# Block-sparse attention and a gated convolution on one core: the first group's output from split words, under a new order of work

## The chip, the cores and the metric

The kernel runs on one core of a Trainium2 chip. The metric is device time in microseconds (us) of one execution; three runs of the kernel before gave 233.24, 233.26 and 234.01, median 233.26. The engines are TensorE (PE, with its weight loads as PEld), VectorE (DVE), ScalarE (ACT), GpSimd (POOL) and SyncE (SP, which issues all DMAs here).

## The reference

Attention over local windows and block summaries, then a gated projection. Four batches, 8 heads of 64, 768 positions; the weights of the second part come as 64-bit floats.

```
k_sum = k.reshape(B, H, nb, 32, D).max(axis=3)
v_sum = v.reshape(B, H, nb, 32, D).mean(axis=3)
scores = concat(local q.k within 16 positions, q.k_sum + log(32)) * scale
x = softmax(scores) @ concat(v, v_sum)          # -> (B, S, H * D)
gate_pre[s] = sum_k conv_w[k] * x[s + k - 4]    # 5 taps along the sequence
out = (sigmoid(gate_pre) * (x @ w_val)) @ w_out
```

## The kernel before, in words

The work is cut into 12 groups `g` (a batch and a third of the sequence, 256 positions, all heads) and 24 units `u` (a group and half of its heads). Unit `u` belongs to group `u // 2`; `r` is 0 or 1, a pair of heads in the unit.

Nothing is scheduled by a planner. A table of words, `ORDER`, is walked once, and each word calls a function that issues a few instructions; every engine takes its own in the order of the table and waits only where an operand isn't ready or a buffer isn't free. The words that matter here, with their engines:

- `W` (PE): a warm-up matmul on zeros, whose result nobody reads. There are 34.
- `Lk`, `Ln`, `Lu`, `Lv`, `Lq`, `Lwv`, `Lwo`, `Lc` (SP): loads. `ks` (DVE) takes key maxima, `kc` (POOL) copies them in between the keys.
- `s` (PE): scores of a unit, 16 matmuls for each `r`. `n` (DVE): mask and row minimum, two score passes. `e` (ACT): two exponentials with row sums. `rr`, `rv` (DVE): row sum and reciprocal. `m` (POOL): normalization. `t` (PE): transposes, `c` (ACT, `cd` on DVE): their copy out of PSUM.
- `x` (PE): attention output. `Y`, `Yd`, `Ya`: its copy to `xf`. `X`, `Xd`, `Xp`: the high word `xh` of `xf` as float32r on ACT, DVE or POOL. `Z` (POOL): the low word `xl = xf - xh`.
- `vp`, `vt`, `vc`, `vb`, `vbc`: value sums of batch 0 (DVE and POOL, into `vpad`), their transposition on PE (`vb_mm`) and the copy. `tv`, `vsp`, `vsc`: the same for later batches.
- `I`, `Id` (ACT or DVE), `T` (DVE), `G` (ACT): the convolution, one start and four taps for each `r`, and the gate (tanh).
- `v` (PE): `val`, x @ w_val. `gf` (DVE): gate times val. `gh`, `ghp` (ACT or POOL) and `gl` (POOL): its high and low word. `o` (PE): the output matmuls; `ob`, `obd`: scaling; `O`: store.
- `rbwo`, `shwo`, `orwo`: a quarter of the 64-bit w_out made into fp32 `wf` (ACT, DVE, DVE). `wcwo`, `wcpwo` (ACT or POOL): its high word as float32r. `wlwo` (POOL): its low word. The same with `wv` for w_val.

A product in split words is three matmuls, high times high, high times low and low times high, each a single pass. `FP32_G = (0,)` makes `val` of group 0, and `FP32_OUT = (0,)` the output of group 0, from fp32 operands instead: `out_mm` then takes `gf` and `wf` and writes one quarter of the sum at a time (`o0.0.0` to `o0.1.3`). The trace shows two records for such a matmul. All three weights of `wf` share one tile: w_out's `wf` overwrites w_val's. `out_mm` in split words takes for each of four `ci` first high times high and high times low, then all four low times high:

```
terms = [(gh(g)[:, ci, rows], w[:, ci, cols]) for ci in range(4) for w in (wh, wl)]
terms += [(gl(g)[:, ci, rows], wh[:, ci, cols]) for ci in range(4)]
```

Of the kernel before, what the change touches and what calls it, by code (L numbers as in the profile page):

```python
# [56 lines left out]
n0.0.1 n0.0.0 ks0.3 Mi kc0.1 kc0.3 cv e0.0.1 e0.0.0 W25 s0.1 W26 W27 W28 W29 W30 n0.1.1 n0.1.0
rbc e0.1.1 e0.1.0 s1.1 shc ks0.2 n1.1.0 rr0 shwv0 rv0 hal0 kc0.2 W31 s1.0 W32 m0.1 e1.1.0 rbwv0
vp1.1 n1.1.1 e1.1.1 n1.0.0 n1.0.1 e1.0.1 t0.1 W33 c0.1 e1.0.0 orwv0 vp0.1 vp1.0 vp0.0 rr1 m0.0
t0.0 vt2.0 vc0.1 vc1.0 vt2.1 s2.1 s2.0 vc0.0 vc1.1 orc rv1 vb0 m1.0 n2.0.0 n2.1.1 n2.0.1 n2.1.0  # L60
c0.0 e2.0.0 e2.0.1 rbwv1 t1.0 e2.1.1 e2.1.0 c1.0 shwv1 vbcd0 orwv1 s3.0 s3.1 rbwv2 Lk1.0 x0.1
x0.0 Y0 m1.1 vt2.2 wcpwv0 wlwv0 t1.1 v0.1.0.0 n3.0.0 n3.1.1 n3.1.0 rr2 shwv2 n3.0.1 orwv2 I0.1
T0.1.0 rv2 T0.1.1 ks1.0 e3.0.0 e3.1.0 I0.0 e3.1.1 e3.0.1 c1.1 vt3.0 vt3.1 vt3.2 vt3.3 vt3.4
vc3.0 vt2.3 vt2.4 vc2.1 m2.1 vc3.1 vc2.0 m2.0 kc1.0 Lq2 s4.1 s4.0 Lwv3 Lv1 Lk1.2 Lk1.1 T0.1.2
n4.0.0 n4.1.0 n4.0.1 T0.0.0 n4.1.1 T0.0.1 shwv3 rr3 v0.0.1.0 v0.1.1.0 vb1 t2.1 e4.1.0 vbc1 s5.1
s5.0 T0.1.3 rv3 n5.1.0 T0.0.2 n5.0.0 T0.0.3 e4.0.0 e4.1.1 c2.1 rbwv3 x1.0 x1.1 Lk1.3 G0 Y1
wcpwv2 I1.1 n5.1.1 orwv3 ks1.2 T1.1.0 n5.0.1 ks1.1 v0.0.0.0 t2.0 c2.0 e4.0.1 m3.1 wcpwv1 m3.0
wlwv1 wlwv2 kc1.1 hal1 wcpwv3 wlwv3 kc1.2 v0.1.1.1 I1.0 v0.1.0.1 v0.0.1.1 t3.1 t3.0 e5.0.0
e5.1.1 c3.1 e5.0.1 c3.0 e5.1.0 Lq3 F1 Lwo1 Lv2 Lu1.2 s6.1 s6.0 Lwo0 Lwo2 Lu1.0 Lq4 F2 x2.1 x2.0
x3.1 x3.0 v0.0.0.1 T1.0.0 rr4 T1.1.1 rv4 T1.0.1 ks1.3 T1.1.2 n6.0.1 T1.0.2 n6.1.0 T1.1.3 n6.0.0  # L70
n6.1.1 Y2 X3 X2 Y3 T1.0.3 shwo1 gf0.0 G1 rbwo1 m4.0 kc1.3 m4.1 Z2 Z3 s7.0 s7.1 t4.0 t4.1 I2.0
I2.1 e6.1.1 gf0.1 n7.0.1 n7.1.1 orwo1 e6.0.1 e7.0.1 rbwo0 c4.1 e6.1.0 c4.0 v1.1.0 v1.0.0 v1.0.1
v1.1.1 rr5 T2.0.0 n7.0.0 T2.1.0 rv5 T2.0.1 n7.1.0 T2.0.2 shwo0 T2.1.1 orwo0 T2.0.3 x4.0 x4.1
rbwo2 e7.1.1 Y4 e7.1.0 s8.1 s8.0 shwo2 T2.1.2 orwo2 T2.1.3 tv1.2 m5.0 tv1.0 m5.1 G2 Ya4 gf1.0
t5.0 Lwo3 Lu1.1 Lk2.0 Lk2.1 Lu1.3 Lv3 o0.0.0 o0.0.1 rbwo3 I3.1 shwo3 orwo3 t5.1 o0.0.2 o0.1.0
o0.0.3 e6.0.0 c5.1 c5.0 T3.1.0 n8.0.0 rr6 n8.1.1 T3.1.1 n8.1.0 n8.0.1 rv6 tv1.3 tv1.1 X4 wcpwo0
Z4 e8.0.0 e7.0.0 rr7 I3.0 ob0.0 x5.0 x5.1 s9.1 s9.0 rv7 Y5 e8.1.0 vsp1 vsc1 e8.0.1 o0.1.1 o0.1.2
o0.1.3 Lk2.2 Lq5 Lk2.3 O0.0 F3 e8.1.1 Lq6 Lv4 Lu2.0 F4 T3.0.0 n9.1.1 T3.0.1 T3.0.2 Ya5 T3.1.2
T3.1.3 T3.0.3 m6.1 m6.0 wcpwo1 m7.1 hal2 X5 Z5 G3 rr8 n9.1.0 rv8 gf1.1 I4.1 T4.1.0 n9.0.0 t7.1
t6.0 wcwo3 I4.0 m7.0 m8.1 c7.1 n9.0.1 c6.0 v2.0.1 v2.1.1 t6.1 c6.1 s10.0 s10.1 x6.0 x6.1 T4.0.0  # L80
T4.0.1 T4.0.2 T4.0.3 T4.1.1 T4.1.2 T4.1.3 gh1.1 e9.0.0 ob0.1 e9.1.1 G4 Y6 I5.0 v2.0.0 v2.1.0
wcpwo2 wlwo0 t7.0 I5.1 c7.0 wlwo3 gl1.1 wlwo1 wlwo2 gh1.0 gl1.0 n10.1.0 n10.1.1 n10.0.0 n10.0.1
Ya6 s11.1 s11.0 x7.1 x7.0 T5.0.0 e10.1.0 e9.0.1 e9.1.0 gf2.0 gh2.0 Y7 T5.0.1 ks2.1 T5.1.0 T5.1.1
T5.0.2 T5.1.2 T5.0.3 rr9 T5.1.3 X6 o1.0 ob1.0 G5 e10.1.1 I6.0 I6.1 e10.0.0 tv2.0 m8.0 ks2.0
kc2.0 kc2.1 hal3 gl2.0 o1.1 n11.0.0 Ya7 X7 gf2.1 T6.1.0 n11.1.1 T6.0.0 n11.1.0 T6.1.1 n11.0.1
t8.1 t8.0 c8.0 c8.1 e10.0.1 e11.0.1 e11.1.1 e11.0.0 ob1.1 ghp2.1 gl2.1 Z7 o2.1 x8.1 s12.1 T6.1.2
T6.0.1 T6.1.3 T6.0.2 rv9 ks2.2 x8.0 s12.0 Y8 e11.1.0 m9.0 hal4 m9.1 Z6 kc2.2 n12.0.0 T6.0.3 G6
Ya8 I7.0 ob2.1 I7.1 rr10 ks2.3 n12.1.0 n12.0.1 n12.1.1 T7.1.0 T7.0.0 rv10 rr11 T7.0.1 T7.1.1
T7.1.2 rv11 T7.1.3 o2.0 t9.0 t9.1 c9.1 c9.0 v3.1.1 kc2.3 x9.1 s13.0 s13.1 x9.0 e12.1.1 Lv5 Lq7
Lu2.1 Lk3.1 Lk3.3 F5 e12.0.0 e12.1.0 Y9 tv2.1 v3.1.0 v3.0.0 n13.1.1 T7.0.2 T7.0.3 G7 I8.1 I8.0  # L90
n13.0.0 n13.0.1 Ya9 n13.1.0 m10.1 m10.0 X9 m11.1 Lu2.2 tv2.2 Xp8 Z8 Z9 t10.1 t10.0 v3.0.1
e12.0.1 c10.1 e13.1.1 gf3.1 T8.0.0 cd10.0 T8.0.1 rr12 T8.1.0 rv12 T8.0.2 T8.0.3 T8.1.1 T8.1.2
T8.1.3 Lu2.3 O0.1 Lv6 s14.1 x10.0 s14.0 x10.1 Y10 ob2.0 gh3.1 hal5 m11.0 gl3.1 tv2.3 gf3.0
n14.0.0 Ya10 G8 I9.1 I9.0 e13.0.0 e13.0.1 n14.0.1 T9.1.0 Xd10 T9.1.1 T9.0.0 n14.1.0 e13.1.0 rr13
T9.0.1 n14.1.1 v4.0.0 v4.0.1 v4.1.0 v4.1.1 rv13 T9.1.2 t11.1 vsp2 t11.0 c11.1 c11.0 s15.1 s15.0
x11.1 x11.0 e14.0.1 vsc2 Y11 ghp3.0 m13.1 gl3.0 m13.0 m12.1 m12.0 gf4.0 T9.1.3 T9.0.2 T9.0.3
# [792 lines left out]
```

## Time and profile before

| | |
|---|---|
| median of 3 runs | 233.26 us (233.24 to 234.01) |
| profiled execution | 233.49 us |
| its span, first to last instruction | 231.7 us |
| PE busy | 224.4 us, 97% |
| DVE busy | 199.7 us, 86% |
| POOL busy | 169.0 us, 73% |
| ACT busy | 165.4 us, 71% |

Busy time counts instructions in flight, so a PE that is busy 97% isn't PE at its peak. A wait is put down to the engine that ended it. Times in the rows count from the first instruction of the execution.

### The profile page before, as it was taken

How to read it: one execution, taken by the hardware profiler on the slowest of the kernel's cores; microseconds unless marked ns; L12 is line 12 of the kernel's file. 1: busy time of each engine (PE TensorE's matmuls, PEld its weight loads, DVE VectorE, ACT ScalarE, POOL GpSimd, SP SyncE). 2: the span in 40 equal slices, each digit the busy share in tenths (PEclk: the TensorE clock that was granted, in tenths of full speed). 3: DMA queues.
4: the chain of work that ended last, by engine and by line, in shares of the span. 5: the costliest groups of instructions: out<-in, count | busy, mean ns of one | idle time of the engine just before them, and what ended most of it. 6: DMA issues, size and time to landing. Idle time of an engine off the chain costs nothing.

```text
span 231.7 us, 8482 instructions
## 1 busy us (share of the span) xinstructions
PE 224.4 (97%) x3210; PEld 191.9 (83%) x3210; DVE 199.7 (86%) x743; ACT 165.4 (71%) x564; POOL 169.0 (73%) x257
## 2 busy tenths in 40 slices
...
GB/s 246 380 419 413 319 335 327 367 305 361 246 315 76 340 271 100 355 312 184 253 94 171 133 171 187 42 11 74 239 143 233 48 141 0 3 0 48 0 226 91
DMA packets 16167, 46.20 MB, mean 199 GB/s; under 512 B 2272, under 2 KB 2528, under 8 KB 16128
## 3 DMA queue, kind: packets, MB, share of 16 engines
...
## 4 chain that ended last, share of the span: by engine, by line
PE 83%; DVE 11%; ACT 3%; issue 1%; POOL 0%; ACTq 0%; DVEq 0%; POOLq 0%
PE out L753 28%; PE val L713 25%; PE s L566 8%; PE pt L618 8%; PE x L629 7%; DVE g L685 4%; PE warm_out L335 3%; DVE sn L581 2%; PE x L647 2%; DVE wf L400 1%; DVE vpad L309 1%; ACT gt L692 1%; DVE ks L258 1%; PE vsp L355 1%; DVE gf L721 1%
## 5 line engine op out<-in xcount | busy, mean ns | idle before, releaser
L685 DVE SCALAR_TENSOR_TENSOR g<-xf,cwt,g 128x256 f32<-128x256 f32 x192 | 93.3, 486 | 7.3 <-ACT g L219 3.0
L594 ACT ACTIVATE p<-sn,nm 128x120 f32<-128x120 f32 x192 | 73.5, 388 | 8.9 <-DVE nm L581 7.6
L608 POOL TENSOR_TENSOR p<-p,ri 128x480 f32<-128x480 f32 x48 | 46.7, 987 | 14.6 <-DVE ri L604 11.6
L713 PE MATMUL val<-xh,wv 128*128 128x256 f32 x352 | 49.6, 284 | 0.0
L581 DVE CUSTOM_DVE_ANT_0 sn<-s,mask 128x120 f32<-128x120 f32 x192 | 43.7, 276 | 3.4 <-PE s L566 3.4
L753 PE MATMUL out<-wo,gh 128*128 128x512 f32 (+1 forms) x184 | 45.8, 390 | 0.3 <-ACT gh L726 0.3
L713 PEld LDWEIGHTS val<-xh,wv 128*128 128x128 f32 x352 | 44.3, 189 | 0.9 <-issue 0.2
L753 PEld LDWEIGHTS out<-wo,gh 128*128 128x128 f32 x184 | 32.4, 188 | 7.3 <-ACT gh L726 0.7
L669 POOL TENSOR_TENSOR xl<-xf,xh 128x512 fp32r<-128x512 f32 x22 | 28.2, 1287 | 12.6 <-ACT xh L656 6.9
L594 ACT ACTIVATION_READ_ACCUMULATOR p<-sn,nm 128x1 f32 x192 | 36.8, 192 | 0.0
L729 POOL TENSOR_TENSOR gl<-gf,gh 128x512 fp32r<-128x512 f32 x22 | 28.2, 1289 | 7.6 <-ACT gh L726 7.3
L621 ACT COPY pts<-pt 120x512 f32<-120x512 f32 x42 | 23.6, 578 | 10.1 <-PE pt L618 10.1
L692 ACT ACTIVATE gt<-g 128x512 f32<-128x512 f32 x24 | 14.3, 597 | 19.7 <-DVE g L685 19.7
L618 PE MATMUL pt<-ident,p 128*120 128x128 f32 x192 | 26.7, 274 | 1.3 <-POOL p L608 1.3
L713 PE MATMUL val<-xl,wv 128*128 128x256 f32 x176 | 27.6, 279 | 0.0
L286 POOL TENSOR_TENSOR vT<-vT 128x384 f32<-128x384 f32 (+3 forms) x44 | 25.0, 569 | 2.9 <-DMA vT<-in_vT_dram 0.3
L618 PEld LDWEIGHTS pt<-ident,p 128*120 128x120 f32 x192 | 21.7, 137 | 5.1 <-POOL p L608 2.2
L753 PE MATMUL out<-wo,gl 128*128 128x512 f32 (+1 forms) x92 | 23.8, 381 | 0.0
L566 PE MATMUL s<-k,q 64*64 64x120 f32 x704 | 23.3, 267 | 0.3 <-DVE g L685 0.3
L713 PEld LDWEIGHTS val<-xl,wv 128*128 128x128 f32 x176 | 23.6, 188 | 0.0
L566 PEld LDWEIGHTS s<-k,q 64*64 64x64 f32 x704 | 18.2, 133 | 3.0 <-issue 2.2
L219 ACT ACTIVATE ob<-out 128x512 f32<-128x512 f32 (+1 forms) x21 | 11.9, 574 | 11.2 <-PE out L753 7.2
...
## 6 DMA issues: line engine op xcount, KB each, us to landing
...
```

Source lines behind the costliest of these rows:

```text
L286: nc.gpsimd.tensor_tensor(dst, src[:, :, :n], src[:, :, n : 2 * n], ALU.add)
L566: nc.tensor.matmul(sp(u)[64 * e : 64 * e + 64, h, c * KW : c * KW + KW], qs[64 * h : 64 * h + 64, i * QT : i * QT + QT], ktile[b, pr][64 * ...
L581: nc.vector.tensor_tensor_reduce(sn(u)[:, n, :], sp(u)[:, h, c * KW : c * KW + KW], mask[:, mv, :], -1.0 / math.sqrt(D), 3.0e38, ALU.add, ...
L594: nc.scalar.activation(pr_(u)[:, n, :], sn(u)[:, n, :], AF.Exp, bias=nm(u)[:, n : n + 1], scale=-1.0, accum_out=rs(u)[:, n, 0:1],)
L608: nc.gpsimd.tensor_tensor(pr_(u)[:, w], pr_(u)[:, w], st["ri", u][:, w].unsqueeze(2).broadcast_to([P, TPU, KW]), ALU.mult,)
L618: nc.tensor.transpose(pt[:KW, i, :], pr_(u)[:, TPU * r + i, :], ident)
L621: (eng or nc.scalar.copy)(pts(u)[:, TPU * r : TPU * r + TPU], st.pop(("pt", u, r))[:KW])
L669: nc.gpsimd.tensor_tensor(xl(g)[:, two(hp), :], xf(g)[:, two(hp), HALO:], xh(g)[:, two(hp), :].bitcast(F32), ALU.subtract,)
L685: nc.vector.scalar_tensor_tensor(gp(u)[:, r], xf(g)[:, pr, o : o + SG], cwt[:, pr, o : o + 1], gp(u)[:, r], ALU.mult, ALU.add,)
L713: nc.tensor.matmul(pp[:, r], w, x, start=first and n == 0, stop=last and n == len(terms) - 1)
L729: nc.gpsimd.tensor_tensor(gl(g)[:, two(cp), :], grp["gf", g, cp], gh(g)[:, two(cp), :].bitcast(F32), ALU.subtract)
L753: nc.tensor.matmul(pp, x, w, start=start and n == 0, stop=stop and n == len(terms) - 1)
```

## The change

`FP32_OUT` becomes empty: the output of group 0 is made by the same 24 matmuls of split words (`o0.0`, `o0.1`) as that of the other groups, and `gh0`, `gl0` and both words of w_out come before it. `val` of group 0 stays in fp32. One new word, `shpwv`, takes the low bits of one quarter of w_val on POOL, with a multiplication by 2^-29 and a minimum in place of a shift. All words of `ORDER` stand in another order; some change engine (three `I` become `Id`, two `Y` become `Yd`, three `ob` become `obd`; `wcwo` is on ACT four times, not once). `v0_sum` gets an argument that no word uses.

```
-FP32_OUT = (0,)
+FP32_OUT = ()
...
 ORDER = """
-ez wz W0 W1 W2 W3 W4 W5 Mu Lk0.0 Lk0.1 Mm ks0.0 ks0.1 kc0.0 W6 W7 W8 W9 W10 W11 W12 W13 W14 W15
-W16 W17 W18 W19 W20 W21 s0.0 W22 W23 W24 Lk0.3 Lk0.2 Lc Lwv0 Ln1 Ln0 Ln2 Lq1 Lwv1 Lv0 Lwv2 Ln3
...
+wz W0 W1 W2 W3 W4 W5 W6 W7 W8 W9 Mu W10 W11 W12 W13 Lk0.0 Lk0.1 Mm ks0.0 ks0.1 ez cv kc0.0 hal0
+s0.0 Lk0.3 Lk0.2 Ln0 Lwv0 Lc Ln2 Ln1 Lq1 Lwv1 Ln3 Lv0 Lwv2 n0.0.0 n0.0.1 ks0.3 kc0.1 kc0.3 Mi
...
-    def v0_sum(i, h):
+    def v0_sum(i, h, n=BLK):
...
     def low_bits(eng, dst, raw):
         low = raw.rearrange("p (n two) -> p two n", two=2)[:, 0]
+        if eng is nc.gpsimd:
+            eng.tensor_scalar(dst.bitcast(U32), low, 2.0**-29, 7.0, ALU.mult, ALU.min)
+            return
         eng.tensor_scalar(dst.bitcast(U32), low, 29, None, ALU.logical_shift_right)
...
-    def w_low(nm, k):
+    def w_low(nm, k, eng=None):
         if wide:
             if nm == "wo":
                 low_put(f"wo{k}", DM, wraw[nm, k])
             else:
-                low_bits(nc.vector, wf[:, k], wraw[nm, k])
+                low_bits(eng or nc.vector, wf[:, k], wraw[nm, k])
...
-        ("wcp", w_head, pcast),
+        ("wcp", w_head, pcast), ("shp", w_low, nc.gpsimd),
```

PE around the output of group 0, before (`s` scores, `pt` transposes, `vsp` the transposed value sums of batch 1):

```order
L566 MATMUL s_977<-k_0_398,q_732 64x120 x8
L618 MATMUL pt_0_1018<-ident,p_684 120x128 x4
L753 MATMUL out_0_1036<-wf,gf_0_803 128x512 x2
L618 MATMUL pt_1_1046<-ident,p_684 120x128 x4
L753 MATMUL out_0_1036<-wf,gf_1_848 128x512
L753 MATMUL out_1_1052<-wf,gf_0_803 128x512
...
L566 MATMUL s_1132<-k_2_519,q_732 64x120 x8
...
L355 MATMUL vsp_1153<-ident,vsT_1_1077 24x128
...
L753 MATMUL out_1_1052<-wf,gf_0_803 128x512
L753 MATMUL out_1_1052<-wf,gf_1_848 128x512 x2
```

The same place on PE in the change:

```order
L632 MATMUL x_1_1067<-pts_1036,v_740 64x64 x2
L756 MATMUL out_0_1112<-wo,gh_784 128x512 x8
L756 MATMUL out_0_1112<-wo,gl_1058 128x512 x4
L569 MATMUL s_1148<-k_3_504,q_975 64x120 x8
L569 MATMUL s_1148<-k_2_506,q_975 64x120 x8
...
L355 MATMUL vsp_1165<-ident,vsT_1_1125 24x128
...
L756 MATMUL out_1_1180<-wo,gh_784 128x512 x8
L756 MATMUL out_1_1180<-wo,gl_1058 128x512 x4
```

The eight fp32 matmuls in three runs have become two runs of twelve; the first stands behind all of `x5`, the second, as before, behind `vsp1`.

POOL at the value sums of batch 1, before (`vT` and `vsT` are sums of values, `p` the normalization, `xl` a low word):

```order
L608 TENSOR_TENSOR p_684<-p_684,ri_919 128x480
L286 TENSOR_TENSOR vT_1_1025<-vT_1_1025 128x24x16
...
L286 TENSOR_TENSOR vsT_1_1077<-vT_1_1025 128x24
L437 CAST wo<-wf 128x512
L669 TENSOR_TENSOR xl_1086<-xf_973,xh_1083 128x512
L608 TENSOR_TENSOR p_845<-p_845,ri_1065 128x480 x2
```

The same place on POOL in the change:

```order
L611 TENSOR_TENSOR p_685<-p_685,ri_773 128x480 x2
...
L732 TENSOR_TENSOR gl_1058<-gf_1_873,gh_784 128x512
L732 TENSOR_TENSOR gl_1058<-gf_0_766,gh_784 128x512
L443 TENSOR_TENSOR wo<-wf,wo 128x512 x4
L286 TENSOR_TENSOR vT_1_981<-vT_1_981 128x24x16
...
L286 TENSOR_TENSOR vsT_1_1125<-vT_1_981 128x24
L659 CAST xh_1109<-xf_973 128x512
L672 TENSOR_TENSOR xl_1196<-xf_973,xh_1109 128x512
```

Two subtractions `gl` and the four subtractions of w_out now stand ahead of the last value sums `vsT_1` (`tv1.1`), which `vsp1` on PE reads.

## Rows read from the trace of the kernel before

**Rows 1.** The page: busy us, share of the span, instructions.

```profile
PE 224.4 (97%) x3210; PEld 191.9 (83%) x3210; DVE 199.7 (86%) x743; ACT 165.4 (71%) x564; POOL 169.0 (73%) x257
```

**Rows 2.** Stretches: their us, busy PE, PEld, DVE, ACT, POOL; clock, DMA.

```profile
9.26:54.29 45.03, 42.78 (x682) 33.74 (x681) 44.09 (x197) 43.04 (x164) 39.30 (x73) 1.00 0.97 355
13.67:54.01 40.34, 38.55 (x629) 31.63 (x626) 39.41 (x172) 38.59 (x143) 37.20 (x67) 1.00 0.96 348
24.80:60.75 35.95, 35.95 (x580) 28.68 (x581) 34.92 (x143) 34.55 (x126) 32.11 (x57) 1.00 0.95 336
60.75:187.91 127.16, 127.16 (x2063) 114.89 (x2062) 119.45 (x448) 98.74 (x337) 103.42 (x142) 1.00 0.55 176
187.91:207.07 19.16, 18.88 (x192) 17.54 (x190) 15.46 (x39) 10.31 (x28) 9.69 (x10) 1.00 0.08 29
```

**Rows 3.** The chain of waits: start us, us, engine and group.

```profile
1.53 6.77 PE warm_out L335 x22
...
24.34 0.43 DVE g L685
24.80 1.05 PE s L566 x32
...
31.75 1.06 PE val L713 x4
...
51.12 1.72 PE out L753 x4
...
53.27 2.61 PE out L753 x6
...
57.80 0.54 PE vsp L355 x4
58.34 2.58 PE out L753 x6
60.91 0.87 PE pt L618 x8
...
64.97 0.98 PE s L566 x32
...
187.91 0.60 ACT ob L219
188.51 0.48 ACT xh L656
188.99 0.77 ACT p L594 x4
```

**Rows 4.** Timeline of DVE: start us, us, instruction, idle time before it.

```profile
8.94 0.28 DVE L581 CUSTOM_DVE_ANT_0 sn<-s,mask 128x120 f32<-128x120 f32 x1 [2.23 <-PE s L566]
```

**Rows 5.** Timelines of ACT and PE at the last wait.

```profile
205.92 0.59 ACT L656 CAST xh<-x 128x512 fp32r<-128x512 f32 x1 [0.61 <-PE val L713]
206.40 0.62 ACT L726 CAST gh<-gf 128x512 fp32r<-128x512 f32 x1
...
207.07 0.50 PE L753 MATMUL out<-wo,gh 128*128 128x512 f32 x1 [0.29 <-ACT gh L726]
```

**Rows 6.** Timelines of PE and POOL at the start.

```profile
1.53 5.04 PE L335 MATMUL warm_out<-warm 128*128 128x512 bf16 x14 [1.53 <-POOL warm L330]
...
5.29 0.44 POOL L272 COPY k<-ks 128x84 f32<-128x84 f32 x2 [3.26 <-DVE ks L258]
```

**Rows 7.** Timeline of POOL: first normalization, last copy in front of `vb1`.

```profile
13.67 1.93 POOL L608 TENSOR_TENSOR p<-p,ri 128x480 f32<-128x480 f32 x2 [0.68 <-DVE ri L604]
...
27.46 0.32 POOL L312 COPY vpad<-vpad 128x12 f32<-128x12 f32 x2
```

**Rows 8.** The chain of waits: 24 output matmuls of split words in a row.

```profile
72.26 5.71 PE out L753 x24
```

**Rows 9.** Groups by line on POOL: busy us, mean ns of one.

```profile
L729 POOL TENSOR_TENSOR gl<-gf,gh 128x512 fp32r<-128x512 f32 x22 | 28.2, 1289 | 7.6 <-ACT gh L726 7.3
...
L440 POOL TENSOR_TENSOR wo<-wf,wo 128x512 fp32r<-128x512 f32 x4 | 5.1, 1294 | 0.0
...
L437 POOL CAST wv<-wf 128x512 fp32r<-128x512 f32 x4 | 2.4, 610 | 0.0
```

**Rows 10.** Timelines of ACT (end of `c5`) and POOL (end of `tv1.1`).

```profile
53.31 1.08 ACT L621 COPY pts<-pt 120x512 f32<-120x512 f32 x2
...
53.78 0.23 POOL L286 TENSOR_TENSOR vsT<-vT 128x24 f32<-128x24 f32 x1
```

More of the change, by code (lines that the diff above doesn't have):

```diff
@@ L54 @@
 ORDER = """
-ez wz W0 W1 W2 W3 W4 W5 Mu Lk0.0 Lk0.1 Mm ks0.0 ks0.1 kc0.0 W6 W7 W8 W9 W10 W11 W12 W13 W14 W15
-W16 W17 W18 W19 W20 W21 s0.0 W22 W23 W24 Lk0.3 Lk0.2 Lc Lwv0 Ln1 Ln0 Ln2 Lq1 Lwv1 Lv0 Lwv2 Ln3
[L57 to L96, printed above, removed]
@@ L127 @@
-v9.0.1 v9.0.0 T19.0.3 n23.0.1 T19.1.0 n23.1.1 e23.1.1 Xd21 rr22 T19.1.1 T19.1.2 T19.1.3 e23.0.1
-G19 Z21 Z20 v9.1.0 v10.0.0 v10.0.1 v9.1.1 gf9.0 I20.0 T20.0.0 T20.0.1 rr23 I20.1 T20.1.0 rv23
-Lv11 F11 O7.0 O8.0 O6.1 ghp9.0 m23.0 t23.0 o8.1 T20.0.2 rv22 m22.1 T20.0.3 T20.1.1 T20.1.2
-T20.1.3 G20 Id21.0 I21.1 gf10.0 c23.0 T21.1.0 T21.0.0 T21.1.1 T21.0.1 T21.0.2 T21.1.2 gf9.1
-T21.1.3 T21.0.3 m23.1 hal11 gl9.0 m22.0 t22.1 t23.1 c22.1 c23.1 v10.1.0 t22.0 c22.0 x23.0 x23.1
-Yd23 X23 Z23 x22.0 x22.1 G21 Yd22 Id22.1 X22 gh9.1 gl9.1 ob8.1 v10.1.1 o9.0 Z22 v11.0.1 T22.1.0
@@ new lines @@
+e0.0.0 e0.0.1 W14 W15 W16 W17 W18 s0.1 W19 W20 W21 W22 n0.1.0 n0.1.1 e0.1.0 e0.1.1 s1.1 ks0.2
+rr0 n1.1.0 rv0 shc shwv0 kc0.2 m0.0 m0.1 W23 s1.0 W24 W25 W26 W27 t0.0 t0.1 W28 W29 W30 n1.0.0
+rbc n1.1.1 n1.0.1 vt2.0 e1.1.0 vp0.1 vp0.0 e1.0.0 e1.0.1 e1.1.1 rbwv0 orc vp1.0 c0.1 rr1 rv1
+vp1.1 orwv0 c0.0 wcwv0 s2.0 s2.1 W31 W32 n2.1.1 n2.0.1 n2.0.0 n2.1.0 vc0.0 vc0.1 vt2.1 vc1.0
+m1.0 m1.1 vc1.1 vt3.0 vt2.2 t1.0 W33 vb0 e2.1.1 rbwv1 e2.0.1 e2.0.0 e2.1.0 c1.0 shwv1 s3.1 s3.0
+rbwv2 vbcd0 x0.0 x0.1 orwv1 n3.0.1 n3.1.1 n3.1.0 rr2 n3.0.0 vt3.1 wlwv0 vt3.2 wcpwv1 vt2.3 vt3.3
@@ new lines @@
+vt2.4 vt3.4 vc2.1 vc3.0 vc3.1 rv2 m2.1 vc2.0 shwv2 Lq2 t1.1 s4.1 s4.0 I0.1 Y0 Id0.0 m2.0 Lwv3
+wlwv1 shpwv3 Lv1 Lk1.0 Lk1.1 Lk1.3 Lk1.2 Lq3 c1.1 e3.1.0 e3.0.1 e3.1.1 v0.0.1.0 vb1 v0.0.0.0
+vbc1 e3.0.0 t2.0 x1.0 T0.0.0 orwv2 T0.1.0 n4.1.1 T0.1.1 n4.0.1 T0.1.2 n4.1.0 T0.0.1 n4.0.0 rr3
+T0.1.3 e4.1.0 e4.0.0 c2.0 rbwv3 e4.0.1 rv3 s5.0 s5.1 x1.1 T0.0.2 ks1.0 T0.0.3 n5.1.1 orwv3
+n5.0.0 G0 wcwv2 m3.1 t3.1 v0.1.1.0 Id1.1 Y1 I1.0 c3.1 e4.1.1 kc1.0 m3.0 wcpwv3 wlwv2 n5.1.0
+ks1.1 wlwv3 hal1 kc1.1 T1.1.0 n5.0.1 rr4 T1.1.1 rv4 m4.1 m4.0 v0.1.0.0 t3.0 t2.1 c3.0 c2.1
@@ new lines @@
+e5.1.0 e5.0.1 e5.1.1 e5.0.0 F1 Lu1.0 Lwo1 v0.0.0.1 v0.0.1.1 x2.0 x2.1 x3.0 x3.1 Lv2 Lwo0 Lu1.2
+Lwo2 s6.0 ks1.3 T1.1.2 ks1.2 T1.1.3 Xd2 gf0.0 T1.0.0 n6.0.1 rr5 T1.0.1 n6.0.0 T1.0.2 shwo1
+T1.0.3 rv5 Y2 gh0.0 Y3 X3 t4.0 v0.1.0.1 c4.0 e6.0.0 rbwo1 tv1.0 kc1.3 kc1.2 v0.1.1.1 s6.1 n6.1.0
+n6.1.1 t4.1 s7.1 s7.0 Z2 Z3 v1.1.1 m5.0 m5.1 tv1.2 G1 gf0.1 orwo1 I2.1 e6.1.1 rbwo0 gh0.1 e6.1.0
+wcwo1 c4.1 e6.0.1 Id2.0 n7.0.1 shwo0 n7.0.0 T2.0.0 orwo0 T2.1.0 n7.1.0 T2.0.1 v1.1.0 v1.0.0
+rbwo2 wcwo0 e7.0.0 F2 x4.1 x4.0 Y4 Lq4 Lwo3 Lu1.3 Lu1.1 shwo2 T2.1.1 orwo2 n7.1.1 T2.1.2 Ya4
```

100 lines of the change are left out of this document (64 added, 36 removed).

## The prediction

> **What bounds the kernel now.** The first view is the busy time by engine [rows 1]: TensorE (PE) is busy 97% of the span, DVE, the next, 86%. That is an average, so the second view is the table by stretch [rows 2]. From 24.80 to 187.91 us PE is busy without a gap (35.95 of 35.95 and 127.16 of 127.16), so there the end moves only if PE gets less work or starts to wait. Up to about 55 us, however, the other three are nearly as full: DVE and ACT are busy 44.09 and 43.04 of 45.03 us, and POOL 37.20 of 40.34 us from 13.67 on. A new order that loads one of them there can make PE wait. After 60.75 they have room (ACT 98.74 and POOL 103.42 of 127.16).
>
> The third view is the chain of waits [rows 3]. It runs over 22 warm-up matmuls, then mostly over DVE, then over PE to 187.91, over ACT and DVE to 207.07, and over PE to the end. Only at its edges does PE stand still: DVE starts its first score pass at 8.94 after 2.23 us of idle time [rows 4], and at 207.07 PE has its one late wait, 0.29 us, for a cast of `gh` on ACT [rows 5].
>
> The profiled execution took 233.49 us with a span of 231.7, so 1.79 lies around the span. The median of the runs is 233.26, which is 0.23 below this execution. All sums are made against 233.49, and 0.23 is taken off at the end.
>
> **The change part by part.**
>
> *Start.* Score piece `s0.0` now stands behind 14 warm-up matmuls, not 22. 22 took 6.77 us and 14 took 5.04 [rows 3, 6], so PE can issue it 1.73 us sooner. Its other condition holds: the key sums are copied in by 5.73 [rows 6], before PE would get there, at 6.5. DVE's first pass moves from 8.94 to about 7.2. That lead doesn't last. DVE now takes `rr0` two steps sooner, so it waits for four exponential pieces at 0.77 us [rows 3], and what ends this stage is POOL. POOL's first `m0` moves from 13.67 to about 11.3 (7.5 for the first exponential, 3.1 for four, 0.7 for the row sum, one score pass and the reciprocal). From there to the last copy into `vpad`, which `vb1` on PE needs, POOL has the same pieces in both orders. It ended them at 27.78 [rows 7] and would now at about 25.4. But PE reaches `vb1` with two `val` pieces fewer behind it, about 1 us each (4 records in 1.06 [rows 3]). Net **-0.5 us** by 26 us. Bounds: -1.73 if all of the lead survives, 0 if none does.
>
> *Out of group 0.* 16 fp32 records go, in three runs of 1.72, 2.61 and 2.58 us: 6.91. 24 matmuls of split words come; such a run took 5.71 [rows 8]. **-1.2 us** on PE. The Trainium skill (TensorE: Matmul & The Clock Gate, Back-to-back issue gap) gives about 131 ns for a matmul of 512 columns in a stream with weight loads. By that 24 would take 3.1 us and this term would be -3.8; the row says 238 ns each, and the row decides.
>
> *What the split words need sooner.* `o0.0` and `o0.1` now need two casts `gh`, two subtractions `gl`, and all four casts and four subtractions of w_out. Before, the subtractions of w_out stood in POOL's row behind all that this output needs. By the order, POOL has this more in front of the end of `tv1.1` (the last value sums that `vsp1` on PE needs): two `gl` at 1.289, four `wlwo` at 1.294, and `shpwv3`; two casts `wcpwv` at 0.61 go to ACT [rows 9]. No row shows `shpwv3`, a one-input pass with an integer source on POOL. The nearest rows are the one-input cast, 0.61, and the two-input subtraction, 1.29; I take 0.61, since it has one input. The Trainium skill (GPSIMD Engine Reference, Elementwise) measured 769 ns for 512 elements in a tight loop; by that this sum would be 0.16 longer. Net +7.15 us. `tv1.1` ended at 54.01 [rows 10]; with the 2.3 us earlier start that makes 58.9 if the 3.14 us of POOL's idle time recur [rows 2], 55.7 if none does, 57.3 for half. The last `wlwo` stands 2.7 us in front: 56.1, 53.0, 54.6.
>
> ACT up to the end of `c5.1` loses one gate (0.60), four `I` (about 0.46 each), one cast and two exponential pieces (1.54), and gets one exponential piece, two `gh` and five weight casts at 0.61: +0.45. It ended at 54.39 [rows 10], so now at 53.1 with its 1.99 us of idle time, 51.1 with none, 52.1 with half. DVE up to `orwo3` gets three `Id` and one `Xd` and loses a `gf`, a tap and a `shwv`: +0.2, so it is not the last of the three.
>
> Now PE with half of the idle times: `x5` ends at 52.65, half a piece after `c5.1`. `o0.0` starts there and would need the last `wlwo` 1.6 us later; it is 0.35 late, so the output ends at 55.9. `s9` takes 0.98, `vsp1` waits from 56.8 to 57.3 and takes 0.54 [rows 3], and `o0.1` takes half of 5.71: 60.7, where PE was at 60.91 before. Of the 1.7 us won, 0.2 is left: **+1.5 us** of new waits. With no idle time they are 0.2; with all of it `o0.1` ends at 62.3, which makes 3.05.
>
> *The middle.* POOL's subtractions of w_out are gone there, and ACT and DVE have the room shown above. DVE gets about 2.9 us more over the whole run (three `Id`, three output scalings, two `Yd`, less two `cd` and one `shwv`) against 7.7 us of idle time from 60.75 to 187.91. **0**; if the cover were gone, up to the 2.9.
>
> *The end.* The 0.29 wait was for a `gh` cast queued on ACT behind cast `X22`. Now `gh9.1` stands ahead of it, so **-0.3**. Next late would be the last `gl` on POOL in front of `o11.1`. The final output, its scaling and its store are unchanged.
>
> Sum: -0.5 - 1.2 + 1.5 - 0.3 = -0.5. 233.49 - 0.5 - 0.23 gives **232.8 us**.
>
> **Rivals.**
>
> *A, the cover holds.* POOL, ACT and DVE go through the first 60 us with next to no idle time, since each waits less for the others once the scores start sooner. The new waits shrink to 0.2: -0.5 - 1.2 + 0.2 - 0.3 = -1.8, 231.5 against the profiled time, **231.2**. If all of the start's lead survives too, 230.0. For it speaks that DVE has under 1 us of idle time in the 45 us of rows 2; against it, that ACT and POOL did wait under a lighter load.
>
> *B, POOL comes late (slower).* POOL's wait times recur in full and `shpwv3` costs 1.29, so `tv1.1` ends at 59.6 and holds back `vsp1`; behind it in PE's row stand `o0.1` and all that follows. New waits 3.05 + 0.7: -0.5 - 1.2 + 3.75 - 0.3 = +1.75, so **235.0**. It decides from the point where `tv1.1` ends behind about 59 us. For it speaks POOL's in-order row with 7 us more; against it, the earlier start.
>
> *C, the late stage.* On DVE the copy `cd23.1` now stands in front of the taps of unit 21 and needs transposes that PE does late. If the gates of units 21 to 23 then come late, PE stalls in front of `o10` or `o11`. DVE is busy 15.46 of 19.16 us there [rows 2], so 3.7 us can go before it costs; about 1 us worse than the forecast, 233.8.
>
> *D, the page's 131 ns for a matmul of 512 columns* would give 230.2. The rows of 238 ns leave it next to nothing.
>
> **How the numbers follow.** About 0.5% (1.17 us) is what a measurement of this kernel can tell from no change. The forecast (half of the waits) has 0.38, A 0.36, B 0.19, C 0.06, D 0.01. A lies below 232.09 but for its edge, and D does too; B lies above 234.43 with C's worst; the rest is within. That gives faster 0.36, same 0.42, slower 0.22. The range reaches from between A's two values, 230.8, to B's 235.0; about 0.1 lies out on each side.
>
> **What would show it.** First score pass on DVE at about 7.2 us; `vb1` on PE at about 25.5; 24 matmuls in 5.7 us for out of group 0, with a gap in front of the last `wlwo` and in front of `vsp1`; PE's second output of group 0 done at 60 to 61; no wait at about 206. Wrong would be: `tv1.1` behind 59 (B), no PE gap from 50 to 60 (A), or PE gaps in the middle, where I have none.

## The result, and the profile after

| | before | the change |
|---|---|---|
| times beside one another | 233.24, 233.26, 233.56, 234.01 us | 234.94, 238.40, 239.39, 239.68 us |
| median | 233.41 us | 238.89 us |
| profiled execution, its span | 233.49, 231.7 us | 234.94, 233.2 us |

The forecast was 232.8 us with a range of 230.8 to 235.0; the median lies outside, on the slow side. The ratio of the undisturbed executions is 1.0129 [1.0081, 1.0177]; it leaves out the two longest, whose clock fell, and since the experiments show that the change itself brings these about, the median says more. What needs explaining is thus two things. Most executions of the change are 3.5 to 6.5 us longer than its shortest. And the shortest are not faster than before: 234.94 beside a median of 233.41 here, 234.47 and 234.60 beside 234.29 in the first experiment, where no difference can be told. The profiled one is the shortest of the four.

Its page, which answers to [rows 1]:

```profile
PE 223.8 (96%) x3218; PEld 194.0 (83%) x3218; DVE 203.6 (87%) x748; ACT 164.3 (70%) x560; POOL 173.4 (74%) x260
```

PE is busy 0.6 us less than before and the span is 1.5 longer, so PE has 2.1 us more of idle time. The table by stretch tells where it lies (us, then busy PE, PEld, DVE, ACT, POOL, then clock, DMA share, GB/s). The first table is of before, the second of the change:

```profile
10.00:20.00 10.00, 8.29 (x131) 5.11 (x135) 9.99 (x56) 9.60 (x44) 8.12 (x17) 1.00 1.03 414
20.00:30.00 10.00, 9.56 (x179) 7.77 (x173) 9.82 (x51) 9.75 (x42) 9.19 (x22) 1.00 0.94 358
30.00:40.00 10.00, 10.00 (x186) 8.99 (x182) 9.96 (x46) 9.29 (x34) 9.67 (x16) 1.00 0.93 320
40.00:50.00 10.00, 10.00 (x176) 9.25 (x178) 9.98 (x38) 9.39 (x32) 8.42 (x13) 1.00 0.98 342
```

```profile
10.00:20.00 10.00, 8.02 (x121) 5.21 (x123) 9.50 (x48) 8.61 (x37) 7.94 (x15) 1.00 1.03 413
20.00:30.00 10.00, 9.15 (x192) 7.75 (x183) 9.49 (x50) 9.59 (x41) 9.91 (x19) 1.00 1.03 416
30.00:40.00 10.00, 9.25 (x150) 7.67 (x143) 9.78 (x33) 9.43 (x35) 9.76 (x16) 1.00 0.95 347
40.00:50.00 10.00, 9.36 (x148) 8.22 (x151) 9.93 (x46) 9.97 (x32) 9.53 (x18) 1.00 0.73 239
```

From 10 to 50 us PE loses 0.27, 0.41, 0.75 and 0.64, together 2.07 us; from 50 to 220 it stands nowhere in this execution, so the late wait of [rows 5] is gone. The steps themselves, from the timelines of DVE, POOL and PE (they answer to [rows 4, 8, 10]):

```profile
7.15 0.28 DVE L584 CUSTOM_DVE_ANT_0 sn<-s,mask 128x120 f32<-128x120 f32 x1
...
28.22 1.99 POOL L393 TENSOR_SCALAR wf<-raw_wv 128x512 uint32<-128x512 uint32 x1
...
55.01 2.11 PE L756 MATMUL out<-wo,gh 128*128 128x512 f32 x8
56.95 1.07 PE L756 MATMUL out<-wo,gl 128*128 128x512 f32 x4
57.95 1.05 PE L569 MATMUL s<-k,q 64*64 64x120 f32 x32
58.94 0.62 PE L355 MATMUL vsp<-ident,vsT 128*24 128x128 f32 x4
59.31 2.09 PE L756 MATMUL out<-wo,gh 128*128 128x512 f32 x8
61.24 1.08 PE L756 MATMUL out<-wo,gl 128*128 128x512 f32 x4
62.16 0.60 PE L621 MATMUL pt<-ident,p 128*120 128x128 f32 x4
```

The first score pass comes 1.79 us sooner, and the output of group 0 takes 2.94 and 2.85 us. But the transposes behind it start at 62.16 where they started at 60.75 [rows 2], and the pass on POOL took 1.99 us. I call this start the mark at 62 us; it measures the early stage by itself. Seven traces are of the change or of variants that differ from it only behind 70 us, and their marks lie at 61.61 to 62.16. So a shift of less than some 0.5 us in a single trace tells nothing, and the early stage is 0.9 to 1.4 us later than in the one trace of before.

**A long execution.** In the first experiment the traced execution was a long one (240.57 us, span 238.9). At 84 us it is 0.38 us ahead of the short one. Then its chain of waits reads:

```profile
84.04 0.44 PE x L632 x26
84.48 2.87 issue
87.35 0.49 PE x L632 x6
87.84 5.42 PE out L756 x12
...
95.67 1.09 PE x L632 x64
```

The short execution at the same place, from its chain of waits:

```profile
84.42 0.47 PE x L632 x32
84.89 2.97 PE out L756 x12
...
90.11 1.09 PE x L632 x64
```

In the long one PE stops inside a run of matmuls, 26 of 32 done, and waits for nothing that another engine or a transfer of data owes it. Then the run of 12 output matmuls takes 5.42 in place of 2.97 us. The stretches of the long execution say why the run takes so long:

```profile
84.00:88.00 4.00, 1.13 (x37) 0.88 (x29) 1.72 (x3) 0.14 (x1) 3.75 (x7) 0.83 1.03 404
88.00:92.00 4.00, 4.00 (x10) 3.13 (x11) 2.78 (x12) 3.09 (x9) 3.92 (x7) 0.50 0.32 125
92.00:96.00 4.00, 4.00 (x47) 3.47 (x50) 3.24 (x14) 2.11 (x9) 0.88 (x3) 0.82 0.46 113
```

PE stood for 2.87 us, and the granted clock behind that is 0.50, the lower of its two levels, 1.2 GHz. Up to the `x` matmuls of unit 9 (95.67 against 90.11) the long execution falls 5.56 us behind, though it was 0.38 ahead at 84: 2.87 in the gap, and the other 3.07 while the clock is low. That is nearly all of the difference of the two spans, 5.7.

### The profile page after: what moved, and what is told of

It reads as the page before. It is cut to its first block, busy times and chain, and to the rows that moved or that the text cites. A ratio compares the mean times of both kernels' runs of the same rounds, so it can differ in the third digit from the quotient of the medians.

```text
span 233.2 us, 8483 instructions
## 1 busy us (share of the span) xinstructions
PE 223.8 (96%) x3218; PEld 194.0 (83%) x3218; DVE 203.6 (87%) x748; ACT 164.3 (70%) x560; POOL 173.4 (74%) x260
## 4 chain that ended last, share of the span: by engine, by line
PE 81%; DMA 9%; ACT 3%; POOL 2%; SPq 2%; issue 1%; DVE 0%; ACTq 0%
PE out L756 29%; PE val L716 28%; DMA raw_wv<-in_wv_dram 8%; PE pt L621 7%; PE x L632 7%; PE s L569 7%; PE x L650 2%; ACT p L597 1%; DMA vT<-in_vT_dram 1%; SPq L369 1%; POOL p L611 1%; SPq L235 1%; POOL vT L286 1%; PE vsp L355 1%; POOL wv L443 1%
## 5 line engine op out<-in xcount | busy, mean ns | idle before, releaser
L716 PE MATMUL val<-xh,wv 128*128 128x256 f32 x352 | 50.3, 286 | 0.0
L756 PE MATMUL out<-wo,gh 128*128 128x512 f32 (+1 forms) x200 | 49.4, 389 | 0.0
L756 PEld LDWEIGHTS out<-wo,gh 128*128 128x128 f32 x200 | 35.3, 188 | 7.0 <-DVE g L688 0.2
L732 POOL TENSOR_TENSOR gl<-gf,gh 128x512 fp32r<-128x512 f32 x24 | 30.9, 1293 | 13.6 <-ACT gh L729 12.9
L624 ACT COPY pts<-pt 120x512 f32<-120x512 f32 x44 | 24.2, 583 | 5.1 <-PE pt L621 5.0
L756 PE MATMUL out<-wo,gl 128*128 128x512 f32 (+1 forms) x100 | 26.0, 382 | 0.0
L756 PEld LDWEIGHTS out<-wo,gl 128*128 128x128 f32 x100 | 18.4, 188 | 3.7
```

The costliest lines, as they stand in the source:

```text
L624: (eng or nc.scalar.copy)(pts(u)[:, TPU * r : TPU * r + TPU], st.pop(("pt", u, r))[:KW])
L716: nc.tensor.matmul(pp[:, r], w, x, start=first and n == 0, stop=last and n == len(terms) - 1)
L732: nc.gpsimd.tensor_tensor(gl(g)[:, two(cp), :], grp["gf", g, cp], gh(g)[:, two(cp), :].bitcast(F32), ALU.subtract)
L756: nc.tensor.matmul(pp, x, w, start=start and n == 0, stop=stop and n == len(terms) - 1)
```

## The experiments

Times in this section are medians with the lowest and highest. Before was run beside each of five sets, each on another chip; it had medians of 233.66 to 234.29 us and took over 237 us in 4 of 73 executions.

**The change again.**

> The changed kernel once more, unaltered. Four executions of it spread over 234.9 to 239.7 us where the kernel before stays within 233.2 to 234.0. Theory P (PE gaps in the first 50 us, always the same): times within 0.5 us of one another, near one of the four values. Theory S (the new order has a race between transfers or a clock that falls in some executions): a spread of several us again, with a granted clock below 1.000 in the long executions; the trace of a long one then shows where it differs from the profile of 234.94.

239.41 us (234.47 to 240.99), two of six below 235. The spread is the change's own, and the trace above is from here. There are long executions at a clock of 1.000 too, such as the 238.40 us above, 3.5 more than the shortest. None of them was traced, so what makes them long is not shown.

**The pass on POOL back to DVE.**

```
-wlwv1 shpwv3 Lv1 ... n4.0.0 rr3
+wlwv1 Lv1 ... n4.0.0 rr3 shwv3
```

> The low bits of quarter 3 of w_val go back from POOL to DVE, behind the row sum of unit 3; all else as in the change. Theory P (POOL's 1.99 us pass, three times what the prediction took, is what PE waits for at 30 to 50 us): POOL is 2 us earlier from 28 us on, the first m of unit 4 ends near 36 and the end comes 1.0 to 1.5 us sooner, 233.4 to 233.9 against the best execution of the change (234.94). Rival D (DVE is as full there): the 0.4 to 1.2 us on DVE delay the taps of group 0 and the score passes of unit 5 by as much, and the time stays within 0.4 us. Theory S: the spread stays in any case.

239.96 us (238.52 to 240.87). The mark moves from 61.77, in the run of the change beside it, to 62.45: with the spread of the marks 0.3 to 0.8 later, and not 1.0 to 1.5 sooner. Theory P falls for this pass; a small delay, as D has it, fits.

**Output of group 0 in fp32.**

```
-FP32_OUT = ()
+FP32_OUT = (0,)
-gh0.0 ... gh0.1 ... gl0.1 gl0.0 ... o0.0 ... o0.1
+o0.0.0 o0.0.1 o0.0.2 o0.0.3 ... o0.1.0 o0.1.1 o0.1.2 o0.1.3
```

> Output of group 0 from fp32 operands again (eight matmuls of two records in each of two runs), with its two gh and two gl left out; the new order, the early splitting of w_out and the low bits on POOL stay. Theory P: the split words are worth their 1.1 us (6.91 against 5.8 us), and POOL loses 2.6 us of gl in front of the value sums of batch 1, which no longer bound: 0.8 to 1.2 us slower than the change in executions of the same kind. Rival W (the early words of w_out and of group 0 are what makes the stage late): equal or up to 1 us faster.

239.91 us (238.50 to 240.75). The mark moves from 61.77 to 62.80: with the spread, the split words are worth 0.6 to 1.2 us. The rival, that the words needed early make the stage late, falls for those of group 0. Those of w_out stand as early here as in the change, so for them it isn't tested.

**The first loads in their former order.**

```
-Ln0 Lwv0 Lc Ln2 Ln1 Lq1
+Lc Lwv0 Ln1 Ln0 Ln2 Lq1
```

> The first loads in the order of before: the convolution weights, the first quarter of w_val and one part of v ahead of the part of v that the change loads first. Theory P: the wait of ACT (0.95 us) and DVE (0.23) for the convolution weights at 12 us goes, but POOL and PE are bound elsewhere, so the time moves by less than 0.4 us. Rival L (the early transfers in another order are the cause of the early gaps and of the spread): 0.5 to 1.5 us faster, and a spread under 1 us like that of the kernel before.

240.06 us (234.58 to 241.20), two of six short; the mark at 61.88 is where it was (61.77). Neither the early loss nor the spread comes from the order of these loads.

**Loads out of the burst.** What PE lacked at 84 us is its own program, as the following rows show. The trace lists 25 transfers of 16 KB on an instruction queue, 0.41 MB, for 3218 matmuls and as many weight loads. Stretches from the start to inside the gap, for the change and for the variant with fewer warm-up matmuls below:

```profile
0.00:87.20 87.20, 78.51 (x1226) 62.55 (x1228) 79.91 (x326) 71.13 (x251) 75.59 (x134) 1.00 0.86 315
```

```profile
0.00:85.50 85.50, 78.27 (x1228) 62.08 (x1228) 79.85 (x327) 72.25 (x254) 74.09 (x133) 1.00 0.88 317
```

In all ten traces with a gap (0.35 to 3.7 us) PE stopped after 1228 weight loads, whatever stood there in the program, as the end of a 16 KB block would make it. The 9th transfer is the one that PE then waits for. By the DMA view of single microseconds it started at 76.4 in the short execution and at 85.1 in the long one. The rows are the microsecond from 76 of the short one, then that from 85 of the long one; the second row of each is the instruction queue:

```profile
q1 hardware_dynamic: 121, 0.35, 95.7%
q8 instruction: 1, 0.02, 6.7%
```

```profile
q1 hardware_dynamic: 101, 0.39, 98.2%
q8 instruction: 1, 0.02, 6.0%
```

PE resumed 2.2 us after that. In front of it SP had handed over, in the long execution (timeline of SP; 478 KB for a `k`, 256 for a store, 1,024 for the two `v`; the first row, `v<-vs`, is the fill `F4`, which copies value sums into `v`):

```profile
75.17 3.33 SPq L369 DMA_DIRECT2D v<-vs  x4
78.53 0.98 SPq L237 DMA_DIRECT2D k<-in_kT_dram  x2
79.56 0.43 SPq L777 DMA_DIRECT2D out_dram<-ob  x1
80.03 0.43 SPq L237 DMA_DIRECT2D k<-in_kT_dram  x1
80.51 1.39 SPq L249 DMA_DIRECT2D v<-in_vw_dram  x2
82.00 0.40 SPq L777 DMA_DIRECT2D out_dram<-ob  x1
```

The rows behind the fill are 3.0 MB, 7 us at the 410 GB/s of that stretch. The kernel before has such a burst as well, 2.9 MB (384 KB for a `vT`, 512 for a `q`):

```profile
73.84 1.61 SPq L249 DMA_DIRECT2D v<-in_vw_dram  x2
75.49 0.43 SPq L230 DMA_DIRECT2D q<-in_qT_dram  x1
76.02 0.38 SPq L242 DMA_DIRECT2D vT<-in_vT_dram  x1
76.44 1.29 SPq L237 DMA_DIRECT2D k<-in_kT_dram  x2
```

But there the 9th transfer had started at 73.3, ahead of the burst. In the first variant 2.0 MB of the 3.0 go later (two `k` and the `v`; the expectation's 1.5 MB is too low):

```
-F4 Lk3.0 Lk2.2 O0.0 Lk3.3 Lv5 O0.1 ... Lu2.3 ob2.1 O2.1 F5
+F4 Lk2.2 O0.0 O0.1 ... Lu2.3 ob2.1 O2.1 Lk3.0 Lv5 Lk3.3 F5
```

> In the change the three loads that stand behind the fill F4 (two k of batch 3 and one v, 1.5 MB) move behind the next output store, in front of F5. Theory F (in long executions PE stands still at 84 us in the middle of a run of x matmuls, 26 of 32 done, with all operands there, because its next 16 KB of instructions come at 85 us instead of 76, behind data transfers; the clock then falls): with 1.5 MB less in front of it the 9th fetch on the instruction queue lands by 78 us, no PE gap of 2.9 us, the clock stays at 1.00, and all executions take 234 to 235 us. Rival C (the gap has another cause, such as a late transfer that x needs): still 238 to 241 us in most executions.

240.87 us (237.30 to 241.51). The transfer started at 82.6 and the gap shrank from 2.87 to 0.67. But the next fill, `F5`, came at 96 and not at 91, and `x` of unit 10 waited 2.7 us at 98 to 102, the clock again falling behind it. The gap moved as theory F has it; the time didn't.

**Fewer warm-up matmuls.**

```
-W23 s1.0 W24 W25 W26 W27 t0.0 t0.1 W28 W29 W30 ... W31 W32 ... W33
+W23 s1.0 W24 W25 t0.0 t0.1
```

> The change without its last eight warm-up matmuls (W26 to W33); the data transfers stand as in the change. PE has 16 instructions fewer in front of every later point, so each block of its instructions is asked for 16 instructions later in the program, about 1 to 2 us. Theory F: the 9th fetch now falls into the quiet stretch of the transfers at 77 to 78.5 us in place of 76, so that the share of long executions (13 of 16 in the change with one load order or the other, and all 12 of the two variants) changes clearly, with no other change of the times than 0.3 us. Rival C: shares as before, 238 to 241 us in most. If PE needs the warm matmuls at 14 to 20 us for its clock, the granted clock falls below 1.00 there.

238.75 us (237.71 to 239.74), none of six short. (The change in its two load orders had 11 long executions of 16, not the 13 of the expectation, so six of six is no clear shift.) I had expected the transfer to move with the program. It started at 85.1 as in the long execution above; the gap, 2.51 us, came behind the same number of weight loads, now inside the output matmuls. The granted clock stayed at 1.00 up to 60 us, so these eight matmuls aren't needed for it.

**The score piece alone, in the kernel before.**

```
-W13 W14 W15 W16 W17 W18 W19 W20 W21 s0.0 W22
+W13 s0.0 W14 W15 W16 W17 W18 W19 W20 W21 W22
```

> The kernel before, with its first score piece s0.0 behind 14 warm-up matmuls in place of 22, and nothing else. It measures the start term alone. If DVE, at 44.09 of 45.03 us, is what bounds the first 50 us, the 1.73 us of lead survive in good part: 0.5 to 1.7 us faster than the kernel before. If loads that land at the same time as ever (weights of the convolution, q, v, w_val) end the waits, the lead is lost by 26 us: within 0.3 us of before.

233.68 us (233.06 to 234.17), ratio 0.9985 [0.9965, 1.0005]: no difference that can be told. The edit doesn't test the start term: the second piece now stood behind 12 warm-up matmuls and came at 10.67, later than in before (9.94). The last experiment moves both.

**The loads ahead of the fill behind it.**

```
-Lq7 Lu2.0 F4 Lk3.0
+F4 Lq7 Lu2.0 Lk3.0
```

> In the change the two loads ahead of fill F4 (q of group 7 and one part of v of batch 2, 0.9 MB) move behind that fill, ahead of the k loads. Theory F with the transfers of 73 to 77 us as those in front of the fetch: the queue is empty when PE asks for its 9th block at 76, the fetch lands at once, and most executions take 234 to 235 us. If it is the transfers from 78.5 us on that hold it back, there are now 0.9 MB more of them: the gap stays in most executions or grows, 238 to 242 us.

239.71 us (234.63 to 241.00), four of twelve below 236. The transfer started at 85.7 and the gap was 3.64. From 72 to 78 us at most 0.06 MB moved in any microsecond, and still the transfer didn't start there: what was handed over ahead of the fill is not what holds it back.

**Loads split around the gap.**

```
-Lq7 Lu2.0 F4 Lk3.0 Lk2.2 O0.0 Lk3.3 Lv5 O0.1 ... Lu2.3 ob2.1
+Lq7 Lu2.0 Lk2.2 F4 O0.0 ... Lu2.3 Lk3.0 Lv5 Lk3.3 O0.1 ob2.1
```

> The change with the same loads in another order around 75 to 90 us: one k load goes ahead of fill F4, the two k and one v of batch 3 and an output store go behind the part of v that waits for the value sums at 85 us, and F5 stays where it is. Between 78 and 83 us some 0.26 MB are handed over in place of 3.0. In the variant with the loads only later, the fetch landed at 82.5 us, as the transfers ran dry, and PE resumed about 2.3 us after a fetch starts, so it has to start by about 82.2. Theory F: the fetch lands at 77 to 81, no gap of PE at 84 us, F5 in time, clock 1.00, 234 to 235 us in all executions. Rival C: 238 to 241 us in most executions, with the gap in the same place.

238.01 us (236.95 to 238.61), a time of the rival's. Yet the transfer started at 76.5 and there is no gap at 84. Now ACT waited for a buffer that the late store `O0.1` held (timeline of ACT), and PE 1.4 us for ACT and F5, with the granted clock at 0.60 from 100 to 104 us:

```profile
96.99 0.60 ACT L215 ACTIVATE ob<-out 128x512 f32<-128x512 f32 x1 [2.17 <-DMA out_dram<-ob]
```

**The fill first.**

```
-Lq7 Lu2.0 F4 Lk3.0 Lk2.2 O0.0 Lk3.3 Lv5 O0.1 ... Lu2.3 ob2.1 O2.1 F5
+Lq7 Lu2.0 Lk2.2 F4 O0.0 ... Lu2.3 Lv5 ob2.1 F5 Lk3.0 O0.1 Lk3.3 O2.1
```

> As the variant with the loads split, but the v of batch 2 and its fill F5 come first at 86 us and the k of batch 3 and the stores behind them. There the fetch came at 76.5 and the gap at 84 us was gone, but F5 was issued at 94.1 in place of 91.1, x of unit 10 waited 1.4 us at 98 and the clock fell behind it, so 237 to 238.6 us. Theory F (the late fetch in the change, and the late fill in my two variants, are separate causes of the same size): with both in time 234.0 to 235.0 us in all executions, clock 1.00. Rival: something else in the transfers or in the clock keeps most executions above 236.5.

242.00 us (239.36 to 242.90), the slowest of all and far from the 234 to 235 expected: the store came later still, ACT waited 5.41 us for it, DVE 2.81 for a `k`, PE 3.45. It has one more reading. No data moved from 81 to 86 us, and yet the instruction transfer started only at 82.5, alone (the microsecond from 82):

```profile
DMA packets 1, 0.02 MB, mean 16 GB/s; under 512 B 0, under 2 KB 0, under 8 KB 0
...
q8 instruction: 1, 0.02, 8.1%
```

So data is not all that holds it back. In the change and its variants it starts at 76.4 or, for a reason that no run here shows, at 82.4 at the earliest, and data in front of it then adds the rest up to 85 or 86. PE's place in its program fits two parts (weight loads counted by stretches from the start). In the four late traces whose queue was empty or had just run dry the transfer started within 0.2 us of PE's 1140th weight load, in the six with the burst 2.5 to 3.3 us behind it, and in the three early ones at the 1107th or 1108th.

**Zeros in place of the low bits** (on top of the last variant; the lowest three bits of a quarter of w_val are left out):

```
-eng.tensor_scalar(dst.bitcast(U32), low, 2.0**-29, 7.0, ALU.mult, ALU.min)
+eng.memset(dst, 0.0)
```

> The variant with the fill in time, and on POOL a plain fill with zeros in place of the low bits of quarter 3 of w_val; the lowest three bits of that quarter are left out. Theory P (POOL's 1.99 us for that pass is what makes PE wait at 33 to 45 us): POOL is 1.4 to 1.8 us earlier from 30 us on, the first transposes behind the output of group 0 start near 60.5 in place of 61.8, and the time is 1.0 to 1.5 us lower than in the variant with the fill in time. Rival D (DVE's row is as late there; moving the pass to DVE cost 0.7): less than 0.5 us lower.

241.32 us (239.74 to 243.69). POOL's 1.99 us became 0.53, and the mark stayed at 61.62, as in the variant with the pass, where theory P wanted 60.5. POOL waited for others at once (its next normalization, timeline of POOL):

```profile
27.75 0.53 POOL L389 MEMSET wf<- 128x512 f32 x1
29.16 0.99 POOL L607 TENSOR_TENSOR p<-p,ri 128x480 f32<-128x480 f32 x1 [0.88 <-ACT p L593]
```

**All transfers in time.** `O0.1` back at 78 us, `v` and F5 first at 86, then the `k` that DVE needs:

```
-Lq7 Lu2.0 F4 Lk3.0 Lk2.2 O0.0 Lk3.3 Lv5 O0.1 ... Lu2.3 ob2.1 O2.1 F5
+Lq7 Lu2.0 Lk2.2 F4 O0.0 O0.1 ... Lu2.3 Lv5 Lk3.0 ob2.1 F5 Lk3.3 O2.1
```

> The change with the two k and one v of batch 3 and 2 taken out of the burst at 78 us, as in my three variants, and this time with nothing that is waited for behind them: both stores of group 0 stay at 78 us (in two variants ACT waited 2.2 and 5.4 us for the second), v and its fill F5 come first at 86 us, then the k that DVE needs at 97 (it waited 2.8 us for it in one variant). Theory F: the instruction fetch lands at 76 to 82.6 us, the gap at 84 us is 0 to 1 us in place of 2.9, no wait at 97 to 102, 234.0 to 236.0 us in all executions. Rival: 238 us and more in most executions, so that the late fetch does not explain the change's median.

236.36 us, all six within 235.99 to 236.77 and at a clock of 1.000; beside before the ratio is 1.0102 [1.0080, 1.0124]. The transfer started at 82.4, at an empty queue, and the list of PE's waits has what is left of it (timeline of PE):

```profile
85.18 0.34 PE L628 MATMUL x<-pts,v 64*64 64x64 f32 x6 [0.89 <-issue]
...
92.94 0.43 PE L565 MATMUL s<-k,q 64*64 64x120 f32 x7 [0.39 <-issue]
```

That shows what makes the long executions: with 0.5 MB in place of 3.0 behind the fill they are gone, and with them 3.0 us of the median (239.41 in the first experiment), or 2.6 if each is taken against before beside it. The burst thus accounts for the transfer's start at 85 to 86 in place of 82.4, for 2.0 of the 2.87 us of the gap, and for the fall of the clock. The other 6 us of lateness, from 76.4 to 82.4, remain. The median also stays above the 236.0 expected. What lies between it and the three short executions of the change (234.47, 234.60 and 234.94), about 1.7 us, is probably for the most part these two gaps, 1.28.

**The early wait for DVE.** Unit 6's second score piece directly behind the first:

```
-s6.0 ... v0.1.1.1 s6.1 n6.1.0 n6.1.1
+s6.0 s6.1 ... n6.0.0 n6.1.0 n6.1.1
```

> The variant with transfers in time, with the second score piece of unit 6 directly behind the first on PE, and its two score passes on DVE ahead of two taps, one low-bits pass and one reciprocal. Theory D (at 43 to 44 us PE waits 0.64 us for DVE, whose passes for unit 6 end 3.3 us later than in before, behind more taps and one cast): the wait goes and the first transposes behind the output of group 0 start 0.5 to 0.7 us sooner than 61.6 to 61.8. Rival P (POOL's value sums and normalizations bound there; a fill with zeros in place of its 1.99 us pass changed nothing, so I do not expect it): 0 to 0.2.

236.65 us (235.38 to 236.88); the mark at 62.16 beside 61.61, so no gain. The 0.64 us at 43 are gone, but three waits for ACT, POOL and DVE, together 1.21, stand at 48 to 52: in this trace, taking one wait out of the early stage moved it to other engines. (What the 0.64 us wait for is itself unsure: the short execution puts it down to DVE, the variant above to a transfer, `v<-vb`.)

**Two parts of the change in the kernel before.**

```
-W13 W14 W15 W16 W17 W18 W19 W20 W21 s0.0 ... W25 s0.1 ... W33
+W13 s0.0 ... W14 W15 W16 W17 W18 s0.1 W19 ... W25
-X22 gh9.1
+gh9.1 X22
```

> The kernel before with two parts of the change by themselves. Start: 14 warm-up matmuls ahead of s0.0, five ahead of s0.1, four ahead of s1.1, as in the change, and the last eight left out. In the variant with s0.0 alone moved, the second score piece stood behind 12 warm-up matmuls and came at 10.67 us, no earlier than in before (9.94), so it could not show the start term. End: the cast gh9.1 stands ahead of X22 on ACT. Theory G (the start's lead of 1.7 us survives where no more work comes with it): 0.5 to 1.5 us faster by the start and 0.3 by the end, 232 to 233 us. Rival (loads that land as late as ever end the waits): start 0, 233.3 to 233.6. If the 16 PE instructions fewer shift its fetches behind a burst of transfers, some executions take 237 us or more.

233.04 us (232.09 to 235.12) beside 234.02 of before, ratio 0.9978 [0.9950, 1.0006]. In the trace the mark is at 59.80, 0.95 ahead of before [rows 2], the wait of [rows 5] is gone, and the span is 230.3, 1.4 less; the traced execution, 232.13 us, is one of the shortest of the twelve. Its median is the lowest here, and at the edge of what theory G has; but the interval just takes in no difference, so it isn't shown to be faster than before.

## Why the prediction was wrong

The step that failed is *the middle*, put at **0** with a bound of 2.9 for lost cover. It looked at what DVE, ACT and POOL had room for and not at what SP hands over there or at how PE gets its instructions. In the new order 3.0 MB are handed over from 78 to 82 us, and in most executions PE's 9th block, due by 84.5, hasn't started ahead of them as it had in before. It then starts at 85 to 86, and in each of the six traces with that burst in front PE stands 2.4 to 3.7 us and its clock falls behind that. The forecast has no term for the clock. The run with all transfers in time undoes 2.6 to 3.0 us of it. None of the rivals was this one, but one of the forecast's own signs of being wrong was: PE gaps in the middle.

The Trainium skill (Runtime: NRT & Kernel Launch, Instruction fetch mechanics) has refills of 16 KiB blocks, which the trace shows, and calls the cost of crossing a boundary mostly hidden; here it was 2.87 us in one place. Its DMA: Bandwidth & Descriptors (Queues, rings and completion order) says that an engine takes turns between queues packet by packet; by that a request would pass a burst quickly, and a start 8.7 us later than in the short execution would mean a late request. The empty queue up to 82.5 fits that; that a burst puts the start off by another 2.5 us or more does not. No run here shows when a request was made.

The other terms, in the order of the forecast:

- *Start, -0.5.* The first pass came at 7.15 as forecast (7.2). In the kernel before, without the rest of the change, the mark comes 0.95 sooner in one trace, with a median that isn't clear of no difference. In the change the lead is lost by 30 us: PE has 0.27 and 0.41 us less of busy time than before in the stretches from 10 and from 20 us.
- *Out of group 0, -1.2.* 5.79 us for 6.91, so -1.1, and 0.6 to 1.2 by the run in fp32: right.
- *New waits, +1.5.* In the short execution PE's idle time up to 60 us rose by 2.0, where start and waits together were to give +1.0. The place was wrong: no gap in front of `o0.0` or `vsp1`, all of it at 10 to 50 us. So rival B's point (POOL's last value sums, done at 59.0) was reached and decided nothing, and the gap-free 50 to 60 us of rival A came with the loss moved ahead of them.
- *`shpwv3`, 0.61, bounds 0.61 to 1.29.* 1.99 us, outside of both; the 769 ns of the Trainium skill's page (GPSIMD Engine Reference, Elementwise) disagree as well. Without the pass the mark stays, so the wrong size cost the forecast nothing.
- *The end, -0.3.* Right as to the wait: PE has none at 206.

What takes the 2 us in the early stage stays open. The runs exclude POOL's pass, the order of the first loads and the split words of group 0. The run with unit 6's scores moved would fit that DVE, ACT and POOL, each over 94% busy from 20 to 50 us, bound it together. There is a rival that no run tests: transfers. The chain of waits of the short execution runs over them for 22 of its first 35 us:

```profile
3.29 8.65 DMA raw_wv<-in_wv_dram
...
12.33 10.24 DMA raw_wv<-in_wv_dram
...
31.17 3.17 DMA vT<-in_vT_dram
```

Some stand early in the chains of all thirteen traces of the new order, and none in the three of the old one. In the tables above the new order moves 416 GB/s from 20 to 30 us, the old one 358.

The reason for the two start times of the transfer, 76.4 and 82.4, is open too. One thing goes with it: the three traces with the early start have the mark at 62.01 to 62.16, those with the late one at 61.52 to 61.88, or at 62.45 and 62.80. Whether that is more than chance isn't shown.
